# Three of four activation chunks transposed by DMA instead of by TensorE, in a fused spectral filter and GEGLU kernel

## The chip, the cores and the metric

The kernel runs on one core of one Trainium2 chip. The metric is the device time of one execution in microseconds (us); the median of three runs of the kernel before is 183.36 us (182.89 to 183.69). The core has five engines that each work through their own list of instructions in order and wait for each other through semaphores: TensorE (PE), ScalarE (ACT), VectorE (DVE), GpSimd (POOL) and SyncE (SP). SP only issues DMA transfers here; ACT issues a few as well.

## The reference, cut to what matters

```python
def _A_ref(x, w_r, w_i):                 # spectral filter
    X = jnp.fft.rfft2(x.astype(jnp.float32), axes=(-2, -1))
    X = X * (w_r + 1j * w_i)
    return jnp.fft.irfft2(X, s=(S, D), axes=(-2, -1)).astype(jnp.bfloat16)

def _B_ref(x, w_gate, w_up, w_down):     # GEGLU
    h = _gelu(jnp.einsum("bsd,df->bsf", x, w_gate)) * jnp.einsum("bsd,df->bsf", x, w_up)
    return jnp.einsum("bsf,fd->bsd", h, w_down)

xn = _layernorm(x, axis=-1)
return x + _A_ref(xn, A_w_r, A_w_i) + _B_ref(xn, B_w_gate, B_w_up, B_w_down)
```

S = 2048 rows, D = 512 columns, 1792 hidden columns; everything is stored as bfloat16.

## The kernel before, in words

The 2048 rows lie in 16 tiles j of 128 rows (one per partition) and 512 columns; four tiles make a chunk m (j = 4m to 4m+3). The layer norm of tile j (`ln_stats`, `ln_rstd`, `ln_apply`, line 425) leaves `xn[:, j, :]` in `bufA`. From there two branches start.

**GEGLU.** The matmuls need the rows on the free axis, so `transposes` (line 432) turns a chunk into `xnT`: for 4 tiles it is 16 TensorE transposes of 128x128 into PSUM (line 444), and then one copy by DVE (line 451) and one by ACT (line 453). `geglu_unit(b, fc)` (line 493) is 4 gate and 4 up matmuls (line 507), a gelu on ACT (line 519) and a product on DVE (line 527) for block b (one chunk of rows) and slice fc of the hidden columns. It waits for all the tiles of its chunk through `ev_xnT`. `down_unit` (line 541) multiplies a finished block by the down weights.

**Spectral branch.** POOL and DVE fold the columns (`half_fold`, `mirror_fold`) into `fold`, which lies in `bufB`. For each j, `unit_A` and `unit_d` do two small matrix products, ACT writes the result `T[:, j, :]` (line 611), which shares `bufA` with `xn`, and SP stores it to a scratch tensor in HBM (`stage_p`, line 613). When eight tiles are stored, `shuffle(q)` (line 616) reads them back in another order, in two transfers each. `unit_B`, `product` (with the two filters `wr_sb` and `wi_sb`), `unit_c`, a second scratch tensor and its read back (`back`), `unit_e` and `unit_fin` follow, and the last adds into `x_sb`.

**Order.** There is no planner: the program is one list written out by hand, and each engine takes its own instructions in the order of that list. `filler()` puts the next GEGLU or down unit between the spectral steps, so that TensorE has work all the time. Block 0 has its first six slices done ahead of the list of fillers. The three fillers ahead of the loop take slices 6 to 8 of block 0, those at j = 0 to 4 slices 9 to 13, and the filler at j = 5 is the first unit of block 1, `geglu_unit(1, 0)`, which is the first to need chunk 2 of the rows (j = 4 to 7). In words of the source, "chunk two" is m = 1, "chunk three" m = 2 and "chunk four" m = 3. The chunks two, three and four are transposed ahead of the loop, at j = 5 and at j = 9.

**The DMA list of SP.** All inputs come first (x, the weights w0 to w3, `small`, `fa`, the down weights `wd_sb` last). The ten transfers of the real filter (`load_filter("wr", ...)`, line 378) stand after the first store of `T` (at j = 1), those of the imaginary filter after the fifth (at j = 5). Of the ten, four bring 16 rows of 16 KB, four bring rows of 514 bytes in mirrored order, and two bring 16 rows of 514 bytes.

Of the kernel before, what the change touches and what calls it, by code (L numbers as in the profile page):

```python
# [7 lines left out]
ACT = mybir.ActivationFunctionType  # L8
# [9 lines left out]
P = 128  # L18
NJ = 16
# [13 lines left out]
def _build_constants():  # L33
# [20 lines left out]
    scale = 1.0 / (S * D)  # L54
    G = np.stack([2.0 * scale * q.T for q in quarters], axis=1)
    G[0, 0] *= 0.5
# [9 lines left out]
    for j in range(NJ):  # L66
# [3 lines left out]
        AM[:, j, 64] = alt  # L70
        EM[0:64, j, :] = 2.0 * np.cos(th.T)
        EM[64:128, j, :] = -2.0 * np.sin(th.T)
        EM[0, j, :] = 1.0
# [48 lines left out]
    for kind in range(2):  # L122
# [5 lines left out]
        for e2 in range(2):  # L128
            if kind == 1 and e2 == 0:
                wt = wi * np.conj(tw).T  # L130
                for base, z in ((0, wi), (2, wt)):
# [20 lines left out]
class _Sched:  # L152
# [14 lines left out]
    def total(self, stream):  # L167
        return (stream, self.stream_cnt[stream])
# [59 lines left out]
def bass_parallel_sum__spectral_gfnet__glu_gated_geglu__prompt_kernel(  # L228
# [19 lines left out]
    sch = _Sched()  # L248

    with ExitStack() as es:  # L250
# [5 lines left out]
        xnT = sb("xnT", [P, NDC, S])  # L256
# [5 lines left out]
        bufB = sb("bufB", [P, 4 * S])  # L262
        bufC = sb("bufC", [P, NG * (NK + 1)])
        tmp = sb("tmp", [P, 8 * NK])
        wr_sb = sb("wr_sb", [P, NG, NK])
        wi_sb = sb("wi_sb", [P, NG, NK])
# [16 lines left out]


        xn = bufA[:, :].rearrange("p (j c) -> p j c", j=NJ)
        T = xn
        ZT = bufA[:, :].rearrange("p (ci j q) -> p ci j q", ci=4, j=NJ)

        fold = bufB[:, :].rearrange("p (t s j d) -> p t s j d", t=2, s=2, j=NJ)
        V = bufB[:, :].rearrange("p (j c) -> p j c", j=NJ)  # L290

        half = bufC[:, 0:NJ * D].rearrange("p (m t j d) -> p m t j d", m=4, t=2, j=4)
# [26 lines left out]
        def sp_bank_bf(slot):  # L319
# [4 lines left out]
        ring_sp = _Ring((3, 4, 5, 6), bank_readers)  # L324
# [3 lines left out]
        ring_tr = _Ring((3, 4), bank_readers)  # L328

        streams = [("pe", 1), ("act", 1), ("dve", 1), ("pool", 1)]  # L330
        streams += [(n, 16) for n in ("x0", "x1", "x2", "x3", "xc1", "xc2", "xc3", "ident", "small", "fa", "eg", "wd", "wr", "wi",
                                      "w0", "w1", "w2", "w3", "dr0", "dr1", "perm1", "jx0", "jx1", "jx2", "jx3", "vd0_0", "vd0_1", "vd0_2", "vd1_0", "vd1_1", "vd1_2", "vd2_0", "vd2_1", "vd2_2", "vd3_0", "vd3_1", "vd3_2", "perm2", "out")]
        for name, inc in streams:
            sem = es.enter_context(nc.semaphore("sem_" + name))
            sch.add_stream(name, sem, inc)
        total = sch.total

        def load(stream, dst, src, eng="sp"):
            sch.op(eng, lambda e: e.dma_start(dst, src), stream=stream)  # L339
            return total(stream)  # L340
# [5 lines left out]
        spec = {}  # L346
# [29 lines left out]
        d2 = nc.dram_tensor("stage_g", [NG, P, NK], BF16).ap()  # L376

        def load_filter(name, dst, src):
            for ri in range(2):
                for e2 in range(2):  # L380
                    plus, minus = (slice(64 * ri + 2 * pm + e2, 64 * ri + 64, 4) for pm in range(2))
                    load(name, dst[plus, :, :], src.rearrange("(c h) k -> c h k", h=P)[:, 32 * e2:32 * e2 + 32, :])

                    g0 = 1 - e2
                    mirror = bass.AP(tensor=src.tensor, offset=src.offset + (P - 32 * e2 - g0) * NK,
                                     ap=[[P * NK, 16], [-NK, NG - g0], [1, NK]])
                    load(name, dst[minus, g0:NG, :], mirror)
                    if e2 == 0:
                        load(name, dst[minus, 0, :], src.rearrange("(c h) k -> c h k", h=P)[:, 64, :])
            spec[name] = [total(name)]  # L390

        def load_eg():
            sch.op("sp", lambda e: e.dma_start(eg[:], c_eg.ap()), deps=[spec["d_last"]], stream="eg")
            spec["eg"] = total("eg")


        ev_zero = sch.op("dve", lambda e: e.memset(hT[1][:, 0, 0:P], 0.0))
# [25 lines left out]
        ev_xn = {}  # L423
# [3 lines left out]
                                                             ALU.subtract, ALU.mult), deps=[ev_rstd[j], ev_ag[j]])  # L427

        ev_xnT = {}
        tr = {}  # L430

        def transposes(a, b, ring, per=2):

            n = (b - a) * P
            evs = []
            for h in range(NDC // per):
                slot, bdeps = ring.alloc(1)
                bank = sp_bank_bf(slot)[:, 0:per * n].rearrange("p (r s) -> p r s", r=per)

                def f_tr(e, h=h, bank=bank):  # L440
                    ins = None
                    for r in range(per):
                        for j in range(a, b):
                            ins = e.transpose(bank[:, r, (j - a) * P:(j - a + 1) * P],  # L444
                                              xn[:, j, (per * h + r) * P:(per * h + r + 1) * P], ident)
                    return ins

                ev_t = sch.op("pe", f_tr, deps=[ev_id] + [ev_xn[j] for j in range(a, b)] + bdeps)
                dst = xnT[:, per * h:per * h + per, a * P:b * P]
                if h % 2 == 0:  # L450
                    ev = sch.op("dve", lambda e, dst=dst, bank=bank: e.tensor_copy(dst, bank), deps=[ev_t])
                else:
                    ev = sch.op("act", lambda e, dst=dst, bank=bank: e.activation(dst, bank, ACT.Copy), deps=[ev_t])
                ring.add_reader(slot, ev)
                evs.append(ev)
            for j in range(a, b):
                ev_xnT[j] = evs
                tr[j] = ev_t

        ev_fold = {}  # L460

        ev_hf = {}

        def half_fold(m):

            rows = xn[:, 4 * m:4 * m + 4, :].rearrange("p j (h d) -> p h j d", h=2)
            deps = [ev_xn[j] for j in range(4 * m, 4 * m + 4)]
            ev_hf[m] = [sch.op("pool", lambda e, t=t, op=op: e.tensor_tensor(half[:, m, t, :, :], rows[:, 0, :, :], rows[:, 1, :, :], op), deps=deps)  # L468
                          for t, op in enumerate((ALU.add, ALU.subtract))]
# [99 lines left out]
        ev_T = {}  # L569
# [27 lines left out]
        def unit_d(j):  # L597
            slot, bdeps = ring_sp.alloc(1)

            def f_d(e):  # L600
                ins = None
                for r in range(4):
                    ins = e.matmul(sp_bank(slot)[:, AT[r] * P:(AT[r] + 1) * P], X1[j % NX1][:, r * P:(r + 1) * P], FD[:, r, :], start=True, stop=True)  # L603
                return ins

            ev_p = sch.op("pe", f_d, deps=[ev_X1[j], ev_fa] + bdeps)
            spec["d_last"] = ev_p
            X1_readers[j % NX1] = ev_p
            dst = T[:, j, :].rearrange("p (h m q) -> p q h m", h=2, q=2)
            src = sp_bank(slot).rearrange("p (h q m) -> p q h m", h=2, q=2)  # L610
            ev_T[j] = sch.op("act", lambda e: e.activation(dst, src, ACT.Copy), deps=[ev_p, tr[j]] + ev_hf[j // 4])  # L611
            ring_sp.add_reader(slot, ev_T[j])
            sch.op("sp", lambda e: e.dma_start(d1[j], T[:, j, :]), deps=[ev_T[j]], stream="dr%d" % (j // 8))
            spec["dr%d" % (j // 8)] = total("dr%d" % (j // 8))
# [86 lines left out]
        ev_ZT = {}  # L701
# [3 lines left out]
        def unit_e(j):  # L705
            slot, bdeps = ring_sp.alloc(1)

            def f_e(e):
                ins = None
                for ci in range(4):  # L710
                    ins = e.matmul(sp_bank(slot)[:, ci * P:(ci + 1) * P], V[:, j, V0[ci]:V0[ci] + HD - 1:2], EM[:, j, :], start=True, stop=True)  # L711
                return ins

            ev_p = sch.op("pe", f_e, deps=[spec["perm2"], spec["eg"]] + bdeps)
            src = sp_bank(slot).rearrange("p (ci q) -> p ci q", ci=4)
            ev_ZT[j] = sch.op("act", lambda e: e.activation(ZT[:, :, j, :], src, ACT.Copy), deps=[ev_p] + [spec["dr%d" % q] for q in range(2)])  # L716
            ring_sp.add_reader(slot, ev_ZT[j])

        ye_readers = [[], []]
# [88 lines left out]
        for j in range(4, 8):  # L808
            ln_apply(j)
        filler(2)  # L810
        transposes(4, 8, ring_tr)
        half_fold(1)

        beside = {
            0: ((ln_stats, 8), (ln_stats, 9)), 1: ((ln_stats, 10),), 2: ((ln_stats, 11), (mirror_fold, 1, 0)),
            3: ((ln_rstd, 8, 12), (mirror_fold, 1, 1)),
            4: tuple((ln_apply, i) for i in range(8, 12)) + ((half_fold, 2),),
            5: ((ln_stats, 12), (ln_stats, 13), (transposes, 8, 12, ring_sp)), 6: ((ln_stats, 14), (mirror_fold, 2, 0)),
            7: ((ln_stats, 15), (ln_rstd, 12, 16), (mirror_fold, 2, 1)),
            8: tuple((ln_apply, i) for i in range(12, 16)) + ((half_fold, 3),), 9: ((transposes, 12, 16, ring_sp),),  # L820
            10: ((mirror_fold, 3, 0), (mirror_fold, 3, 1), (clear_holes,), (shuffle, 0)),
        }
        for j in range(NJ):
            filler()
            unit_A(j)
            if j >= 1:
                unit_d(j - 1)
            if j == 1:
                load_filter("wr", wr_sb, A_w_r)
            if j == 5:  # L830
                load_filter("wi", wi_sb, A_w_i)
            for f, *args in beside.get(j, ()):
                f(*args)
        filler()
# [83 lines left out]
```

## Time and profile before

| | |
|---|---|
| median of 3 runs | 183.36 us |
| the profiled execution, its own time | 182.99 us |
| its span in the profile | 181.2 us |
| PE busy | 175.1 us of the span |
| DVE, ACT, POOL busy | 117.3, 88.5, 55.5 us |
| moved by DMA | 26.10 MB |
| granted TensorE clock | 1.00 |

The profile is of one execution on the chip; "span" is the time from its first to its last instruction, and the device time has 1.8 us around it. PE busy 97% of the span means that nearly everything else lies beside matmuls. "To landing" is the time from the issue of a transfer until its data has arrived.

### The profile page before, as it was taken

How to read it: one execution, taken by the hardware profiler on the slowest of the kernel's cores; microseconds unless marked ns; L12 is line 12 of the kernel's file. 1: busy time of each engine (PE TensorE's matmuls, PEld its weight loads, DVE VectorE, ACT ScalarE, POOL GpSimd, SP SyncE). 2: the span in 40 equal slices, each digit the busy share in tenths (PEclk: the TensorE clock that was granted, in tenths of full speed). 3: DMA queues.
4: the chain of work that ended last, by engine and by line, in shares of the span. 5: the costliest groups of instructions: out<-in, count | busy, mean ns of one | idle time of the engine just before them, and what ended most of it. 6: DMA issues, size and time to landing. Idle time of an engine off the chain costs nothing.

```text
span 181.2 us, 3176 instructions
## 1 busy us (share of the span) xinstructions
PE 175.1 (97%) x1148; PEld 99.8 (55%) x1168; DVE 117.3 (65%) x252; ACT 88.5 (49%) x161; POOL 55.5 (31%) x54
## 2 busy tenths in 40 slices
PE   7889999999999999999999999999999999999994
PEld 7778555565655554455455554444555555555453
DVE  3758958799675545538678585933266758886431
ACT  2744357777463542166576574523363636663000
POOL 0082290373630000000000000000049679997900
PEclk9999999999999999999999999999999999999999
DMA  5999970999999585723436858475001121110101
GB/s 153 354 364 374 371 250 30 187 195 195 208 205 201 156 257 157 220 58 98 112 87 131 204 113 215 103 168 116 5 0 58 37 75 36 58 60 5 58 29 58
DMA packets 32224, 26.10 MB, mean 144 GB/s; under 512 B 2256, under 2 KB 31440, under 8 KB 32080
## 3 DMA queue, kind: packets, MB, share of 16 engines
q1 hardware_dynamic: 28368, 23.90, 50.2%
q10 hardware_dynamic: 3840, 2.00, 5.3%
q8 instruction: 9, 0.15, 0.4%
q14 instruction: 7, 0.06, 0.1%
HBM read 17.48 MB, written 6.30 MB: 131 GB/s over the span
## 4 chain that ended last, share of the span: by engine, by line
PE 90%; DMA 4%; DVE 3%; SPq 1%; issue 1%
PE ps L507 50%; PE ps L555 27%; DMA wu_sb<-in_B_w_up_dram 4%; PE ps L577 2%; PE ps L732 2%; PE ps L711 2%; PE ps L603 2%; PE ps L649 2%; PE ps L680 2%; PE ps L444 2%; SPq L339 1%; DVE hT L527 1%; DVE tmp L666 1%; DVE tmp L668 0%; DVE JX L667 0%
## 5 line engine op out<-in xcount | busy, mean ns | idle before, releaser
L507 PE MATMUL ps<-xnT,wu_sb 128*128 128x512 bf16 (+1 forms) x246 | 58.3, 358 | 0.1
L507 PE MATMUL ps<-xnT,wg_sb 128*128 128x512 bf16 (+1 forms) x234 | 56.2, 357 | 1.3 <-DMA wu_sb<-in_B_w_up_dram 0.5
L527 DVE TENSOR_TENSOR hT<-ps,gg 128x512 bf16<-128x512 f32 (+1 forms) x62 | 39.5, 638 | 21.7 <-PE ps L507 20.5
L555 PE MATMUL ps<-wd_sb,hT 128*128 128x512 bf16 (+1 forms) x234 | 50.3, 366 | 0.2
L519 ACT ACTIVATE gg<-ps 128x512 bf16<-128x512 f32 (+1 forms) x62 | 34.4, 555 | 25.4 <-PE ps L507 24.3
L746 POOL TENSOR_TENSOR bufC<-bufC 128x256 bf16<-128x256 f32 x16 | 14.7, 917 | 85.5 <-DVE bufC L743 85.5
L507 PEld LDWEIGHTS ps<-xnT,wu_sb 128*128 128x128 bf16 x248 | 24.2, 98 | 24.2
L555 PEld LDWEIGHTS ps<-wd_sb,hT 128*128 128x128 bf16 x238 | 22.9, 98 | 22.6
L507 PEld LDWEIGHTS ps<-xnT,wg_sb 128*128 128x128 bf16 x248 | 22.9, 98 | 16.0 <-DMA wu_sb<-in_B_w_up_dram 0.7
L561 DVE TENSOR_TENSOR x_sb<-ps,x_sb 128x512 bf16<-128x512 f32 (+1 forms) x17 | 11.2, 660 | 28.7 <-PE ps L555 28.7
L750 POOL TENSOR_TENSOR x_sb<-x_sb,bufC 128x512 bf16<-128x512 bf16 x16 | 18.7, 1170 | 2.3
L468 POOL TENSOR_TENSOR bufC<-bufA 128x1024 bf16<-128x1024 bf16 x8 | 16.8, 2125 | 7.9 <-DVE bufA L426 7.9
L611 ACT ACTIVATE bufA<-ps 128x512 bf16<-128x512 f32 x16 | 11.9, 744 | 9.2 <-PE ps L603 9.2
L685 ACT ACTIVATE Vp<-ps 128x514 bf16<-128x514 f32 x16 | 9.6, 599 | 13.6 <-PE ps L680 13.6
L716 ACT ACTIVATE bufA<-ps 128x512 bf16<-128x512 f32 x16 | 9.4, 597 | 13.5 <-PE ps L711 13.5
L403 DVE BATCH_NORM_STATS2 st<-x_sb 128x6 f32<-128x512 bf16 x16 | 10.9, 678 | 2.2 <-DMA x_sb<-in_A_x_dram 2.2
L742 DVE TENSOR_TENSOR bufC<-bufC,ps 128x256 f32<-128x256 f32 x16 | 6.7, 421 | 5.3 <-ACT bufC L739 5.3
L654 ACT ACTIVATE Xc<-ps 128x514 bf16<-128x514 f32 x12 | 7.0, 595 | 4.0 <-PE ps L649 4.0
L418 POOL TENSOR_SCALAR rstd<-ag 128x4 f32<-128x4 f32 (+1 forms) x4 | 1.6, 402 | 20.2 <-DVE ag L404 20.2
L584 ACT ACTIVATE tmp<-ps 128x512 bf16<-128x512 f32 x9 | 5.4, 597 | 4.5 <-PE ps L577 4.5
L739 ACT ACTIVATE bufC<-ps 128x256 f32<-128x256 f32 x16 | 6.0, 378 | 2.6 <-PE ps L732 2.6
L746 DVE TENSOR_TENSOR bufC<-bufC 128x256 bf16<-128x256 f32 x16 | 6.8, 425 | 0.5
(46 smaller groups left out, 144.1 us busy)
## 6 DMA issues: line engine op xcount, KB each, us to landing
stage_g<-Vp SPq DMA_DIRECT2D x16, 128.5 KB, 2.8
stage_p<-bufA SPq DMA_DIRECT2D x16, 128.0 KB, 7.5
bufC<-stage_p SPq DMA_DIRECT2D x4, 512.0 KB, 5.1
out_dram<-x_sb SPq DMA_DIRECT2D x15, 128.0 KB, 1.7
wd_sb<-in_B_w_down_dram SPq DMA_DIRECT2D x1, 1792.0 KB, 14.0
wr_sb<-in_A_w_r_dram SPq DMA_DIRECT2D x6, 257.0 KB, 6.5
wi_sb<-in_A_w_i_dram SPq DMA_DIRECT2D x6, 257.0 KB, 11.0
JX<-Xc SPq DMA_DIRECT2D x24, 64.2 KB, 2.3
```

The lines of the kernel that those rows point to most:

```text
L403: ev = sch.op("dve", lambda e: e.bn_stats(st[:, j, :], x_sb[:, j, :]), deps=[ev_x[j]])
L468: ev_hf[m] = [sch.op("pool", lambda e, t=t, op=op: e.tensor_tensor(half[:, m, t, :, :], rows[:, 0, :, :], rows[:, 1, :, :], op), deps=deps ...
L507: ins = e.matmul(gu_bank(slot)[:, 0:w], wsb[:, dc, fc * P:(fc + 1) * P], xnT[:, dc, b * 512 + a:b * 512 + a + w], start=(dc == 0), stop=(d ...
L519: ev_gg = sch.op("act", lambda e: e.activation(gg, gu_bank(gslot)[:, 0:w], ACT.Gelu_apprx_tanh), deps=[ev_gm] + gg_readers[s2])
L527: ev_h = sch.op("dve", lambda e: e.tensor_tensor(hT[hb][:, fc, a:a + w], gu_bank(uslot)[:, 0:w], gg, ALU.mult), deps=[ev_um, ev_gg] + hdeps)
L555: ins = e.matmul(bank(slot)[:, 0:w], hT[hb][:, fc, jj * P:(jj + 1) * P], wd_sb[:, fc, cs], start=(fc == 0), stop=(fc == NFC - 1))
L561: ev_a = sch.op("dve", lambda e, slot=slot, cs=cs: e.tensor_tensor(x_sb[:, j, cs], bank(slot)[:, 0:w], x_sb[:, j, cs], ALU.add), deps=[ev_ ...
L611: ev_T[j] = sch.op("act", lambda e: e.activation(dst, src, ACT.Copy), deps=[ev_p, tr[j]] + ev_hf[j // 4])
L685: ev_v = sch.op("act", lambda e: e.activation(Vp[sv][:], sp_pair(slot), ACT.Copy), deps=[ev_p] + Vp_readers[sv])
L716: ev_ZT[j] = sch.op("act", lambda e: e.activation(ZT[:, :, j, :], src, ACT.Copy), deps=[ev_p] + [spec["dr%d" % q] for q in range(2)])
L746: y = [sch.op(("dve", "pool")[h], lambda e, h=h, op=op: e.tensor_tensor(rS[s2][:, h * HD:(h + 1) * HD], yeS[s2][:, 0, :], yeS[s2][:, 1, :] ...
L750: ev_o = sch.op("pool", lambda e: e.tensor_tensor(x_sb[:, j, :], x_sb[:, j, :], rS[s2], ALU.add), deps=[a, b, ev_xn[j]] + ev_acc.get(j, []))
```

## The change

The chunks two to four are no longer transposed by TensorE but by DMA transfers that SP issues, one for each tile of 128x512, from `xn` to `xnT`. The first four stand ahead of the loop, where the 16 TensorE transposes of chunk two stood. The others are spread over j = 5 to 10, so that all twelve are issued ahead of `shuffle(0)`. Chunk one stays on TensorE.

`T` moves from `bufA` to `bufB`, where each tile takes the place of the folded tile that `unit_A` has read, and the order of dimensions of `fold` changes to make the two match. With it the wait of the `T` write for the transposes and the folds goes away. The final `ZT`, still in `bufA`, waits for the transfers of the three chunks instead of for the stores.

The real filter is loaded directly behind the down weights, in place of after the first store of `T`; the imaginary filter's ten transfers follow the first four transposes, two at each j from 0 to 4.

```diff
-        fold = bufB[:, :].rearrange("p (t s j d) -> p t s j d", t=2, s=2, j=NJ)
+        fold = bufB[:, :].rearrange("p (j t s d) -> p t s j d", t=2, s=2, j=NJ)
+        T = bufB[:, :].rearrange("p (j c) -> p j c", j=NJ)
...
+        for _ in load_filter("wr", wr_sb, A_w_r):
+            pass
...
+        def transfers(a, b):
+
+            for j in range(a, b):
+                sch.op("sp", lambda e, j=j: e.dma_start(xnT[:, :, j * P:(j + 1) * P], xn[:, j, :], transpose=True),
+                       deps=[ev_xn[j]], stream="tr%d" % (a // 4))
+            for j in range(a, b):
+                ev_xnT[j] = [total("tr%d" % (a // 4))]
...
-            ev_T[j] = sch.op("act", lambda e: e.activation(dst, src, ACT.Copy), deps=[ev_p, tr[j]] + ev_hf[j // 4])
+            ev_T[j] = sch.op("act", lambda e: e.activation(dst, src, ACT.Copy), deps=[ev_p])
...
-            ev_ZT[j] = ...  deps=[ev_p] + [spec["dr%d" % q] for q in range(2)])
+            ev_ZT[j] = ...  deps=[ev_p] + [ev_xnT[i][0] for i in (7, 11, 15)])
...
-        transposes(4, 8, ring_tr)
+        transfers(4, 8)
         half_fold(1)
+        filter_i = load_filter("wi", wi_sb, A_w_i)
...
-            5: ((ln_stats, 12), (ln_stats, 13), (transposes, 8, 12, ring_sp)), 6: ((ln_stats, 14), (mirror_fold, 2, 0)),
-            7: ((ln_stats, 15), (ln_rstd, 12, 16), (mirror_fold, 2, 1)),
-            8: tuple((ln_apply, i) for i in range(12, 16)) + ((half_fold, 3),), 9: ((transposes, 12, 16, ring_sp),),
-            10: ((mirror_fold, 3, 0), (mirror_fold, 3, 1), (clear_holes,), (shuffle, 0)),
+            5: ((ln_stats, 12), (ln_stats, 13), (transfers, 8, 9)), 6: ((ln_stats, 14), (mirror_fold, 2, 0), (transfers, 9, 10)),
+            7: ((mirror_fold, 2, 1), (ln_stats, 15), (ln_rstd, 12, 16), (transfers, 10, 11)),
+            8: tuple((ln_apply, i) for i in range(12, 16)) + ((half_fold, 3), (transfers, 11, 12)),
+            9: ((transfers, 12, 14),), 10: ((transfers, 14, 16), (mirror_fold, 3, 0), (mirror_fold, 3, 1), (clear_holes,), (shuffle, 0)),
...
-            if j == 1:
-                load_filter("wr", wr_sb, A_w_r)
-            if j == 5:
-                load_filter("wi", wi_sb, A_w_i)
+            for _ in range(2):
+                next(filter_i, None)
```

`load_filter` becomes a generator that yields after each transfer. The list of SP in the changed kernel reads: inputs, down weights, ten transfers of the real filter, four transposing transfers, then the imaginary filter and the stores of `T` in turn, the remaining eight transposing transfers between the stores of j = 4 to 9, `shuffle(0)`, the last six stores, `shuffle(1)`.

More of the change, by code (lines that the diff above doesn't have):

```diff
@@ L285, in bass_parallel_sum__spectral_gfnet__glu_gated_geglu__prompt_kernel @@
         xn = bufA[:, :].rearrange("p (j c) -> p j c", j=NJ)
-        T = xn
         ZT = bufA[:, :].rearrange("p (ci j q) -> p ci j q", ci=4, j=NJ)
-        fold = bufB[:, :].rearrange("p (t s j d) -> p t s j d", t=2, s=2, j=NJ)
+        fold = bufB[:, :].rearrange("p (j t s d) -> p t s j d", t=2, s=2, j=NJ)
+        T = bufB[:, :].rearrange("p (j c) -> p j c", j=NJ)
         V = bufB[:, :].rearrange("p (j c) -> p j c", j=NJ)
@@ L331, in bass_parallel_sum__spectral_gfnet__glu_gated_geglu__prompt_kernel @@
         streams += [(n, 16) for n in ("x0", "x1", "x2", "x3", "xc1", "xc2", "xc3", "ident", "small", "fa", "eg", "wd", "wr", "wi",
-                                      "w0", "w1", "w2", "w3", "dr0", "dr1", "perm1", "jx0", "jx1", "jx2", "jx3", "vd0_0", "vd0_1", "vd0_2", "vd1_0", "vd1_1", "vd1_2", "vd2_0", "vd2_1", "vd2_2", "vd3_0", "vd3_1", "vd3_2", "perm2", "out")]
+                                      "w0", "w1", "w2", "w3", "dr0", "dr1", "perm1", "jx0", "jx1", "jx2", "jx3", "vd0_0", "vd0_1", "vd0_2", "vd1_0", "vd1_1", "vd1_2", "vd2_0", "vd2_1", "vd2_2", "vd3_0", "vd3_1", "vd3_2", "perm2", "tr1", "tr2", "tr3", "out")]
         for name, inc in streams:
@@ L382, in load_filter @@
                     load(name, dst[plus, :, :], src.rearrange("(c h) k -> c h k", h=P)[:, 32 * e2:32 * e2 + 32, :])
+                    yield
                     g0 = 1 - e2
@@ L387, in load_filter @@
                     load(name, dst[minus, g0:NG, :], mirror)
+                    spec[name] = [total(name)]
+                    yield
                     if e2 == 0:
                         load(name, dst[minus, 0, :], src.rearrange("(c h) k -> c h k", h=P)[:, 64, :])
-            spec[name] = [total(name)]
+                        yield
         def load_eg():
@@ L429, in bass_parallel_sum__spectral_gfnet__glu_gated_geglu__prompt_kernel @@
         ev_xnT = {}
-        tr = {}
         def transposes(a, b, ring, per=2):
@@ L457, in transposes @@
                 ev_xnT[j] = evs
-                tr[j] = ev_t
+        def transfers(a, b):
[4 more added lines that the diff above has]
+                ev_xnT[j] = [total("tr%d" % (a // 4))]
         ev_fold = {}
@@ L715, in unit_e @@
             src = sp_bank(slot).rearrange("p (ci q) -> p ci q", ci=4)
-            ev_ZT[j] = sch.op("act", lambda e: e.activation(ZT[:, :, j, :], src, ACT.Copy), deps=[ev_p] + [spec["dr%d" % q] for q in range(2)])
+            ev_ZT[j] = sch.op("act", lambda e: e.activation(ZT[:, :, j, :], src, ACT.Copy), deps=[ev_p] + [ev_xnT[i][0] for i in (7, 11, 15)])
             ring_sp.add_reader(slot, ev_ZT[j])
```

## The prediction

> **What bounds the kernel now.** I read the page's busy times first, then the chain that ended last, piece by piece in order of time.
>
> ```profile
> PE 175.1 (97%) x1148; PEld 99.8 (55%) x1168; DVE 117.3 (65%) x252; ACT 88.5 (49%) x161; POOL 55.5 (31%) x54
> ...
> PE 90%; DMA 4%; DVE 3%; SPq 1%; issue 1%
> ...
> 23.97 0.89 PE ps L444 x16
> ...
> 37.68 0.89 PE ps L444 x16
> ...
> 48.74 0.89 PE ps L444 x16
> ```
>
> TensorE is the bound, 97% of the span, and 90% of the last chain is its work. The three bottom lines (start, length) are the transposes of chunks two, three and four: they stand on the path themselves. Whatever leaves TensorE shortens the time, and whatever makes it wait lengthens it, for there is no slack behind it.
>
> Next is when the first unit of block 1 starts, which is the first reader of chunk two. The timeline of TensorE has the fillers of j = 0 to 4 up to 34.9 us, and then:
>
> ```profile
> 34.90 0.39 PE L577 MATMUL ps<-fa,bufB 128*128 128x128 bf16 x4
> 35.12 0.39 PE L603 MATMUL ps<-fa,tmp 128*128 128x128 bf16 x4
> 35.34 1.03 PE L507 MATMUL ps<-xnT,wg_sb 128*128 128x512 bf16 x4
> ```
>
> The last line is `geglu_unit(1, 0)`. Then the transfers: SP's issues by the timeline, the DMA share (second to last column) and rate in GB/s (last) by stretches, and times to landing.
>
> ```profile
> 13.84 0.44 SPq L339 DMA_DIRECT2D wd_sb<-in_B_w_down_dram  x1
> 30.06 0.32 SPq L613 DMA_DIRECT2D stage_p<-bufA  x1
> 30.42 6.45 SPq L339 DMA_DIRECT2D wr_sb<-in_A_w_r_dram  x10
> 36.91 2.17 SPq L613 DMA_DIRECT2D stage_p<-bufA  x4
> ...
> wd_sb<-in_B_w_down_dram SPq DMA_DIRECT2D x1, 1792.0 KB, 14.0
> ...
> 25.00:26.00 1.00, 1.00 (x7) 0.41 (x6) 0.30 (x1) 1.00 (x2) 1.00 (x2) 1.00 0.85 267
> 26.00:27.00 1.00, 0.95 (x8) 0.61 (x8) 0.37 (x1) 0.56 (x2) 1.00 (x1) 1.00 0.14 44
> ...
> 34.00:36.00 2.00, 2.00 (x17) 1.14 (x16) 1.11 (x3) 1.51 (x4) 0.04 (x1) 1.00 1.09 170
> ...
> wr_sb<-in_A_w_r_dram SPq DMA_DIRECT2D x1, 257.0 KB, 9.0
> stage_p<-bufA SPq DMA_DIRECT2D x1, 128.0 KB, 8.3
> ```
>
> The down weights land at 13.84 + 14.0 = 27.8 us, and the engines fall idle at about 26.1. The filter then moves at only 170 GB/s, though the share is 1.09 (packets in flight overlap, so it can pass 1): the engines are not short of work but slow at this work. The last two lines belong to the tenth filter transfer, issued at 36.3, and to the store issued next, at 36.91: they land at 45.3 and 45.2. A lone store of that size, the one of 30.06, lands in 1.7 us by its own window. So a transfer waits behind everything issued ahead of it on SP's queue.
>
> How long does a filter occupy the queue? The first transfer of `wr_sb` lands at 30.42 + 3.8 = 34.2, the tenth at 45.3, so nine take 11.1 us. By the windows around each issue the 16 KB-row kind follows its predecessor by about 1.0 us, the mirrored one by about 1.7, the 8 KB one by about 0.6. With 1.0 for the first, a filter costs 12.1 us of queue. The imaginary one confirms it, though it had stood in the queue for 8 us when its turn came: behind stores that end at 38.6 + 7.7 = 46.3, its last lands at 46.1 + 12.4 = 58.5, or 12.2 us.
>
> **The change, part by part.**
>
> *Transposes taken from TensorE.* 48 instructions in three pieces of 0.89 us, all on the path: 3 x 0.89 = -2.67 us. Three copies each of DVE (about 0.68) and ACT (1.02) go too; both engines are idle a third of the time or more and end no long wait of TensorE, so 0.
>
> *`T` to `bufB`, `fold` reordered.* The `T` copy (744 ns) keeps its shape; the eight `mirror_fold` (674 ns) write runs of 128 in place of 512. If that doubled them, 0.7 us each would still fit, since DVE waited 20.5 us in all for TensorE ahead of its products. 0. The waits that the `T` write loses had long ended.
>
> *Real filter moved up.* It fills the gap between 26.1 and 30.4 us. Its ten issues (about 0.6 us each) go out by 13.84 + 0.44 + 6.45 = 20.7 if the queue takes them, ahead of the readiness of chunk two: DVE writes tiles 4 to 7 from 21.54 to 22.9. But the transposes of chunk two are now behind the filter in the queue. The filter runs from 26.1 and its last transfer lands at 27.8 + 12.1 = 39.9 us. Before, TensorE had chunk two at 24.9 and read it from 35.34; with the first piece of 0.89 gone it wants it at 34.45. **The filter alone lands 5.45 us too late.**
>
> *The twelve transposing transfers.* The trace shows none. Each moves 128 KB within SBUF. The lower bound is a plain store of that size: the four of 36.91 land between 45.2 and 46.3, so 0.37 us each. The nearest small-piece row is the mirrored filter transfer: 16 x 31.5 rows of 514 bytes, 31.5 for each of 16 engines, in 1.7 us, or 54 ns a piece. A 128x512 tile in 128-column pieces is 512 pieces of 256 bytes, 32 an engine. At half a piece's time (by bytes) it is 0.87 us, at a whole one 1.73. I take the middle, 1.3 us. Above these, the 8 KB transfer holds the queue 0.6 us with a single piece per engine; if each of the four 128-column groups paid that, it is 2.4 us. Moving single elements at 54 ns would be 65,536 / 16 x 54 ns = 221 us each; I think that excluded for a transfer that is told to transpose, and give it 1 in 100.
>
> At 1.3 us the fourth lands at 39.9 + 5.2 = 45.1, and TensorE waits 45.1 - 34.45 = **+10.65 us**. With 0.37 it is 6.9, with 2.4 it is 15.05. SP's own issue of a transpose is also unknown, but the first four have 15 us (22.9 to 38) of cover while the filter drains.
>
> Two rules of the Trainium skill disagree here, and no run so far shows the operation. "VectorE: DVE Perf Modes", The three transpose paths, gives 1309 ns for one 128x128 by DMA against 390 ns on TensorE (here 55.6 ns in a stream); four blocks in a row would be an estimated 5.2 us a transfer and a time near 212 us. "Advanced Engine Details and Errata", X-Bar Transpose (TRN2), says that such transfers are as fast as regular ones, which is the 0.37 us row and 189.6 us.
>
> *A cold restart.* At the start, after idleness, the 50 warm-up matmuls of 128x128 took 4.81 us, while 16 transposes of that size take 0.89, 55.6 ns each. So 4.81 - 2.78 = 2.0 us went to a slow start, though the granted clock reads 1.00. Whether a wait of 10 us in the middle brings it back the trace doesn't show: bounds 0 and 2.0. I take **+2.0**, the only row of a start after idleness.
>
> The skill's "TensorE: Matmul & The Clock Gate", Why this matters for your kernels, warns of gaps over about 3 us, after which the clock is halved again. It would make the full 2.0 of this wait, and nothing of a wait under 3.
>
> *What is late next.* Behind the waiting unit on TensorE stand `unit_A(5)` and `unit_d(4)`, hence the store of tile 4 on SP, and with it the transfers of chunks three and four. Chunk three is read at block 2's start, some 18 fillers later (about 79 us before), chunk four at block 3's: covered by over 15 us. The tighter one is `shuffle(1)`: issued at 68.43, its second half landed at 75.5, and `unit_B` began at 76.98: 1.5 us of slack. At 1.3 us a transfer the queue holds chunk two to 43.4, the imaginary filter and four stores to 57.1, eight transposes and six stores (10.4 + 2.2) to 69.7, `shuffle(0)` (5.1 - 1.7 = 3.4) to 73.1. The last `T` is then written at 66.7 - 2.67 + 10.65 + 2.0 = 76.7, so its store finds the queue free. +0.
>
> **Sum.** 182.99 - 2.67 + 10.65 + 2.0 = 192.97 us for the profiled execution; its time lies 0.37 under the median, so 193.3 us.
>
> **Rivals.**
>
> *Slow transposes, a second wait.* At 2.4 us each the first wait is 15.05 us, and the queue is behind: chunk two to 47.8, filter and stores to 61.4, eight transposes and six stores to 82.8, `shuffle(0)` to 86.2, six stores land at 90.1, `shuffle(1)` 7.1 us later at 97.2. `unit_B` would be due at 76.98 - 2.67 + 15.05 + 2.0 = 91.4: 5.8 us more. 183.36 - 2.67 + 15.05 + 2.0 + 5.8 = 203.5. It begins near 2 us a transfer. For it: nothing measured; against it: the mirrored row. 0.20.
>
> *Faster.* The filter follows the weights at their rate (350 GB/s between 22 and 25 us): 2.05 MB in 5.9 us, landed at 33.7, transposes of 0.37 us at 35.2, a wait of 0.7: 183.36 - 2.67 + 0.7 = 181.4. It decides from chunk two landing before 34.45 + 2.67 = 37.1. Against it: both filters took 12 us with nothing else to slow them. It could also come about if transposes overtake in the queue; the store behind the filter did not. 0.07.
>
> *No change.* Chunk two at about 37.1 us; it needs half of each of these errors. 0.03.
>
> **How the numbers follow.** The forecast has 0.70, with its own range from 187.6 (0.37 us, no cold start) to 197. The range goes from 186.5, a filter that takes 11 us as well, to 205, to take in most of the slow rival. Less than 0.5% either way can't be told from no change. Faster 0.07, same 0.03, slower 0.90.
>
> **What would show it.** Right: a wait of some 7 to 12 us on TensorE at about 34.5 us, ended by the transfers into `xnT`; real filter landing near 40; every later stage shifted by the net amount, with matmuls after the wait at twice their time for 2 to 4 us. Wrong: chunk two landed by 37 us; transposes far from 1.3 us apart; or a second wait at the first `unit_B`.

## The result, and the profile after

The changed kernel takes 190.16 us (median of 4 runs, 189.64 to 190.69) against 183.36 us for the kernel before (median of 3 runs; a fourth took 312.61 us): a ratio of 1.0374 with a 95% interval of 1.032 to 1.0428. Here and below, medians and ranges are over all runs of a kernel but for that one, while ratios leave out runs over 1.5% above the kernel's fastest. The prediction was 193.3 us, slower.

The page of the changed kernel first, with the lines that answer to those shown of before.

```profile
span 187.9 us, 3106 instructions
...
PE 175.6 (93%) x1120; PEld 98.0 (52%) x1120; DVE 115.5 (61%) x249; ACT 85.9 (46%) x158; POOL 55.1 (29%) x54
...
PE 88%; DVE 5%; DMA 3%; SPq 2%; issue 1%; ACT 0%
```

48 transposes are gone (1168 weight loads before, 1120 now), and TensorE's share fell from 97% to 93%. The two busy times, 175.1 and 175.6 us, can't be compared: the page of before shows only 1148 matmuls beside its 1168 weight loads, so about 20 records are missing there. The timeline of TensorE shows where (start, length, instructions, and in brackets the idle time ahead with what ended it).

```profile
34.33 0.39 PE L616 MATMUL ps<-fa,tmp 128*128 128x128 bf16 x4
42.09 1.89 PE L520 MATMUL ps<-xnT,wg_sb 128*128 128x512 bf16 x4 [7.37 <-DMA xnT<-bufA]
43.77 1.91 PE L520 MATMUL ps<-xnT,wu_sb 128*128 128x512 bf16 x4
45.48 0.63 PE L590 MATMUL ps<-fa,bufB 128*128 128x128 bf16 x4
45.91 0.43 PE L616 MATMUL ps<-fa,tmp 128*128 128x128 bf16 x4
46.18 1.03 PE L520 MATMUL ps<-xnT,wg_sb 128*128 128x512 bf16 x4
47.04 1.03 PE L520 MATMUL ps<-xnT,wu_sb 128*128 128x512 bf16 x4
47.90 0.39 PE L590 MATMUL ps<-fa,bufB 128*128 128x128 bf16 x4
48.13 0.39 PE L616 MATMUL ps<-fa,tmp 128*128 128x128 bf16 x4
48.35 1.03 PE L520 MATMUL ps<-xnT,wg_sb 128*128 128x512 bf16 x4
```

The first unit of block 1 waits 7.37 us for chunk two. From its start to the start of the next unit it is 46.18 - 42.09 = 4.09 us; the one behind that takes 48.35 - 46.18 = 2.17. So 1.92 us more go to slow matmuls. The windows show why (the number after the engines' is the granted clock, then DMA share and GB/s).

```profile
36.00:38.00 2.00, 0.00 (x0) 0.00 (x0) 0.29 (x1) 0.00 (x0) 1.63 (x1) 1.00 1.30 151
38.00:40.00 2.00, 0.00 (x0) 0.00 (x0) 0.00 (x0) 0.00 (x0) 2.00 (x2) 0.79 1.56 74
...
42.00:44.00 2.00, 1.91 (x5) 0.74 (x6) 0.00 (x0) 0.00 (x0) 0.00 (x0) 0.50 0.96 200
44.00:46.00 2.00, 2.00 (x9) 0.97 (x8) 0.28 (x1) 0.60 (x1) 0.00 (x0) 0.50 1.25 246
46.00:48.00 2.00, 2.00 (x16) 1.06 (x14) 1.93 (x5) 1.69 (x3) 0.00 (x0) 1.00 1.04 230
```

The clock falls to half after about 4.4 us of waiting and comes back about 4 us after work resumes. Together: 7.37 + 1.92 - 2.67 = 6.62 us; the span grew by 187.9 - 181.2 = 6.7. Only 0.1 us is left over. SP's issues in the timeline, the time to landing of the last filter transfer, and the chain of waits over the end of the wait:

```profile
14.20 14.61 SPq L339 DMA_DIRECT2D wr_sb<-in_A_w_r_dram  x10
28.85 11.69 SPq L468 DMA_TRANSPOSE xnT<-bufA  x4
40.59 1.23 SPq L339 DMA_DIRECT2D wi_sb<-in_A_w_i_dram  x2
...
wr_sb<-in_A_w_r_dram SPq DMA_DIRECT2D x1, 257.0 KB, 11.9
```

```profile
36.30 0.79 SPq L468
37.09 0.04 issue
37.14 2.10 SPq L468
39.23 0.04 issue
39.28 2.77 DMA xnT<-bufA
42.05 0.05 issue
42.09 1.03 PE ps L520 x2
```

The ten filter transfers keep SP until 28.8 us, not 20.7, and the four transposes until 40.5: SP is held up. It doesn't wait for data, since DVE had written chunk two by 23.0 us. That it waits until the queue has room is the likely reading, but the trace doesn't name what it waits for. The last filter transfer, issued at 28.2, lands 11.9 us later, at 40.1; the last transpose lands at 42.05.

### The profile page after: what moved, and what is told of

It reads as the page before. It is cut to its first block, busy times and chain, and to the rows that moved or that the text cites. A ratio compares the mean times of both kernels' runs of the same rounds, so it can differ in the third digit from the quotient of the medians.

```text
span 187.9 us, 3106 instructions
## 1 busy us (share of the span) xinstructions
PE 175.6 (93%) x1120; PEld 98.0 (52%) x1120; DVE 115.5 (61%) x249; ACT 85.9 (46%) x158; POOL 55.1 (29%) x54
## 2 busy tenths in 40 slices
DMA packets 38752, 27.67 MB, mean 147 GB/s; under 512 B 8784, under 2 KB 37968, under 8 KB 38608
## 4 chain that ended last, share of the span: by engine, by line
PE 88%; DVE 5%; DMA 3%; SPq 2%; issue 1%; ACT 0%
PE ps L520 51%; PE ps L568 26%; PE ps L745 2%; PE ps L724 2%; PE ps L590 2%; PE ps L662 2%; PE ps L616 2%; PE ps L693 2%; DMA x_sb<-in_A_x_dram 2%; SPq L468 2%; DMA xnT<-bufA 1%; DVE hT L540 1%; DVE bufA L433 1%; DVE st L410 1%; DVE tmp L679 1%
## 5 line engine op out<-in xcount | busy, mean ns | idle before, releaser
L520 PE MATMUL ps<-xnT,wg_sb 128*128 128x512 bf16 (+1 forms) x248 | 59.4, 362 | 7.5 <-DMA xnT<-bufA 7.4
L520 PE MATMUL ps<-xnT,wu_sb 128*128 128x512 bf16 (+1 forms) x248 | 59.4, 362 | 0.0
L540 DVE TENSOR_TENSOR hT<-ps,gg 128x512 bf16<-128x512 f32 (+1 forms) x62 | 39.4, 637 | 29.5 <-PE ps L520 28.1
L624 ACT ACTIVATE bufB<-ps 128x512 bf16<-128x512 f32 x16 | 11.9, 743 | 9.2 <-PE ps L616 9.2
L729 ACT ACTIVATE bufA<-ps 128x512 bf16<-128x512 f32 x16 | 9.4, 597 | 13.4 <-PE ps L724 13.4
L590 PEld LDWEIGHTS ps<-fa,bufB 128*128 128x128 bf16 x64 | 5.1, 101 | 4.1 <-issue 0.6
```

What stands on the lines that cost most here:

```text
L520: ins = e.matmul(gu_bank(slot)[:, 0:w], wsb[:, dc, fc * P:(fc + 1) * P], xnT[:, dc, b * 512 + a:b * 512 + a + w], start=(dc == 0), stop=(d ...
L540: ev_h = sch.op("dve", lambda e: e.tensor_tensor(hT[hb][:, fc, a:a + w], gu_bank(uslot)[:, 0:w], gg, ALU.mult), deps=[ev_um, ev_gg] + hdeps)
```

## The experiments

The theory after the result: chunk two waits because the filter's 2.05 MB stand ahead of it on SP's queue. Four kernels were made to test it, all run on one chip beside the kernel before (183.06 us).

**Filters back where they were, transposes by DMA.**

```diff
-        for _ in load_filter("wr", wr_sb, A_w_r):
-            pass
...
-            for _ in range(2):
-                next(filter_i, None)
+            for at, name, dst, src in ((1, "wr", wr_sb, A_w_r), (5, "wi", wi_sb, A_w_i)):
+                if j == at:
+                    for _ in load_filter(name, dst, src):
+                        pass
```

> Queue theory (chunk two waits because the real filter's 2.05 MB stand ahead of it on SP's queue): with both filters loaded where they were before the change, the four transposing transfers run directly behind the down weights, at about 0.5 us each, and land by 30 us; TensorE wants them at 34.7, so the wait of 7.4 us and the slow matmuls after it (1.9 us) are gone and the three pieces of 0.89 us stay saved: 183.4 - 2.7 = 180.7 us. Rival (transposing transfers are slow in themselves, some 3 us each as the 11.7 us of SP's issue suggests): chunk two lands at 37 to 39, a wait of 2 to 4 us stays, 183 to 185 us.

Measured: 191.22 us, ratio 1.0442 (1.0406 to 1.0479). The wait for chunk two is gone, as expected (it landed at 32.05 us, not by 30, and was wanted at 34.7), but the gain didn't come. TensorE's waits in this kernel:

```profile
PE ps L658 <- DMA bufC<-stage_p: 7.7, 1, 7.7
```

Line 658 is `unit_B`: it now waits 7.7 us for `shuffle(1)`, and the clock reads 0.50 after that too. There is a second wait that the first had hidden.

**The real filter's move alone**, on the kernel before.

```diff
-            if j == 1:
-                load_filter("wr", wr_sb, A_w_r)
...
+        load_filter("wr", wr_sb, A_w_r)
+
         def load_eg():
```

> The kernel before with nothing changed but the real filter loaded behind the down weights (all transposes on TensorE). Queue theory: no reader on the path waits for anything behind the filter, so 183.4 us within 0.5%, with the filter landing near 40 us. Rival (the filter's loads themselves disturb the stream of weights, which land at 29.6 in place of 27.8): above 185 us.

Measured: 183.12 us, ratio 1.0005 (0.9995 to 1.0015). The move costs nothing by itself; it needs a reader behind it.

**Chunk two alone back on TensorE.**

```diff
-        transfers(4, 8)
+        transposes(4, 8, ring_tr)
```

> The changed kernel with chunk two alone back on TensorE; chunks three and four stay with the transfers, the real filter stays behind the down weights. Queue theory: no wait at 34.7 us, two pieces of 0.89 us saved: 183.4 - 1.8 = 181.6 us. Rival (the eight later transfers also cost, through SP's queue and the shuffle): 183 us or more, with a wait at the first unit_B.

Measured: 182.74 us, ratio 0.9985 (0.9969 to 1.0001): between the two expectations. There is no wait at 34.7 us, but 1.2 us at the first `unit_B`. The rival was right that the eight later transfers cost something.

**Chunk two's transposes and the real filter swapped on SP's list**, nothing else.

```diff
         transfers(4, 8)
+        for _ in load_filter("wr", wr_sb, A_w_r):
+            pass
         half_fold(1)
```

> The changed kernel with the four transposing transfers of chunk two and the ten transfers of the real filter swapped on SP's list, nothing else. Queue theory: as with the filters put back, 180.7 us, with the real filter landing near 42 us and nobody waiting for it. Rival (slow transposes): 183 to 185 us. Rival (early filter harms by itself): above the time with the filters put back by 1 us or more.

Measured: 190.29 us (187.94 to 191.19), ratio 1.0315 (1.026 to 1.037). Of the waits, the one for chunk two is gone, and one of 5.0 us stands at `unit_B`. That settles the first wait: order on the queue alone makes or removes it. The profile is of the shortest of the four runs, so in the others the second wait may have been longer. The second is seen in SP's list, here the kernel before and then the swapped one (the two halves of `shuffle(0)`, the last six stores of `T`, `shuffle(1)`):

```profile
59.42 1.30 SPq L622 DMA_DIRECT2D bufC<-stage_p  x2
60.77 6.28 SPq L613 DMA_DIRECT2D stage_p<-bufA  x6
68.43 1.24 SPq L622 DMA_DIRECT2D bufC<-stage_p  x2
```

```profile
49.05 2.98 SPq L464 DMA_TRANSPOSE xnT<-bufA  x1
...
61.95 2.50 SPq L464 DMA_TRANSPOSE xnT<-bufA  x2
64.58 2.12 SPq L631 DMA_DIRECT2D bufC<-stage_p  x2
66.74 5.11 SPq L622 DMA_DIRECT2D stage_p<-bufB  x6
73.97 1.23 SPq L631 DMA_DIRECT2D bufC<-stage_p  x2
```

`shuffle(0)` goes out 5.2 us later, and `shuffle(1)`, which needs the last stores, 5.5 us later. The last `T` was written at 64.7 us, but its store left SP only at 71.42 (in the kernel before 66.69 and 66.72), so the delay stands on SP's list. TensorE wanted the data at 75.2 and could start at 80.1. A transposing transfer takes SP 1.2 us where a store takes about 0.6. Two explanations: SP's own time (theory S), or the load on the queue and the DMA engines (theory D). Four more kernels, beside 183.3 us of the kernel before:

**Chunk four's transfers behind `shuffle(1)`**, chunk two ahead of the filter.

```diff
-            9: ((transfers, 12, 14),), 10: ((transfers, 14, 16), (mirror_fold, 3, 0), ...
+            10: ((mirror_fold, 3, 0), ...
...
         shuffle(1)
+        transfers(12, 16)
         load_eg()
```

> The kernel with chunk two's transfers ahead of the real filter, and chunk four's four transfers moved behind shuffle(1), where SP is free and 30 us remain until they are read. Theory S (the second wait, 5.0 us at the first unit_B, comes from SP's own time: 1.25 us to issue a transposing transfer, twelve of them ahead of the last store of T and of shuffle(1)): four fewer ahead take 5 us off SP, shuffle(1) goes out near 69 us and the wait falls to 0 to 1 us: 180.7 to 181.7 us. Rival D (the DMA engines are behind with the bytes, the filters above all): the eight transposes moved 1 MB only, the wait stays at 4 us or more, 186 us.

Measured: 184.6 us with a wide spread (182.55 to 187.07), ratio 1.0052 (1.002 to 1.0083). In the profiled execution (183.03 us) `shuffle(0)` goes out at 59.60 us and the wait at `unit_B` is gone. But the four transposes hold SP for 7.14 us from 69.81, the transfers into `JX` behind them go out late, and `unit_c` waits 1.74 us. The wait at `unit_B` went as theory S expected and not as rival D did, and the time fits neither. It doesn't decide between the two, since four transfers fewer are also 0.5 MB less on the queue. The other runs took 1.6 us more in the median, which this profile doesn't explain.

**Plain copies in place of the eight later transposes** (the transposition of chunks three and four is left out).

```diff
-                sch.op("sp", ... e.dma_start(xnT[:, :, j * P:(j + 1) * P], xn[:, j, :], transpose=True),
+                src = xn[:, j, :] if j < 8 else xn[:, j, :].rearrange("p (r s) -> p r s", r=NDC)
+                sch.op("sp", ... e.dma_start(..., src, transpose=True) if j < 8 else e.dma_start(..., src),
```

> The kernel with chunk two's transfers ahead of the real filter, but the eight transfers of chunks three and four are plain copies of the same 128x512 elements in the same 256-byte pieces to the same place: the transposition of 1024 rows is left out. Theory S: a plain issue takes SP about 0.58 us in place of 1.25, 8 x 0.67 = 5.4 us less ahead of shuffle(1), and the wait at the first unit_B is gone: 180.7 us. Rival D (bytes and pieces on the DMA engines): the same load, so the wait stays at 4 us or more and the time at 186 us or above.

Measured: 186.59 us, ratio 1.0178 (1.012 to 1.0237). The wait stays:

```profile
PE ps L659 <- DMA bufC<-stage_p: 4.8, 1, 4.8
...
62.35 1.32 SPq L632 DMA_DIRECT2D bufC<-stage_p  x2
63.71 5.87 SPq L623 DMA_DIRECT2D stage_p<-bufB  x6
72.89 1.23 SPq L632 DMA_DIRECT2D bufC<-stage_p  x2
```

SP reaches `shuffle(0)` only 2.2 us earlier than with transposes, though eight issues at half the time should have saved about 5, and `shuffle(1)` 1.1 us earlier. Theory S, as the whole cause, falls: the same bytes in the same pieces, not transposed, make nearly the same wait.

**Idle matmuls during the wait**, on the changed kernel: 125 of 128x128, whose result nobody uses.

```diff
+            if j == 5:
+                keep_warm(125)
             filler()
```

> The changed kernel with 125 idle matmuls of 128x128 (7 us at 55.6 ns, their result is not used) put on TensorE just ahead of the unit that waits for chunk two. Theory (the clock falls to half after the wait of 7.4 us, which costs 1.9 us): the granted clock stays at 1.00, the eight matmuls of the unit take 1.73 us in place of 3.4, and the time falls by 1.9 us to about 188.3 us. Rival (the matmuls are slow because of the transfers into the same memory, not because of the idle time): no gain, 190.2 us or above.

Measured: 191.5 us, ratio 1.0443 (1.0385 to 1.0501): no gain, so the expectation failed. The timeline says why:

```profile
34.73 7.14 PE L843 MATMUL ps<-hT 128*128 128x128 bf16 x125
44.26 1.04 PE L520 MATMUL ps<-xnT,wg_sb 128*128 128x512 bf16 x4 [2.38 <-DMA xnT<-bufA]
45.13 1.59 PE L520 MATMUL ps<-xnT,wu_sb 128*128 128x512 bf16 x4
...
47.36 1.77 PE L520 MATMUL ps<-xnT,wg_sb 128*128 128x512 bf16 x4
48.97 1.03 PE L520 MATMUL ps<-xnT,wu_sb 128*128 128x512 bf16 x4
```

Chunk two landed 2.2 us later in this execution, and 2.38 us of idleness were left. Of the 2.2 us, 0.7 are the filter's (landed at 40.82) and 1.5 the third transpose's, which came 2.0 us behind the second (on this see the last section). The unit starts at full speed, and the clock falls to 0.50 a microsecond into it, for about 3.5 us. The slow phase came all the same, only later: this unit and the next take 6.02 us, to 50.28, in place of 4.34, so 1.7 us are lost. The rival (transfers slow the matmuls) isn't supported: the first four ran at full speed, and in the kernel with the filters put back the clock reads 0.50 after a wait with no transposing transfer near it. What the warm clock is worth was not isolated; the 1.92 us are read from the trace.

**Chunks two and four by DMA, chunk three on TensorE**, filters as before the change.

```diff
-            5: (..., (transfers, 8, 9)), 6: (..., (transfers, 9, 10)), 7: (..., (transfers, 10, 11)),
+            5: (..., (transposes, 8, 12, ring_sp)), 6: (...), 7: (...),
...
         shuffle(1)
+        transfers(12, 16)
```

> Filters where they were before the change, chunk two by transfers directly behind the down weights, chunk four by transfers behind shuffle(1), chunk three on TensorE. No transfer stands between the stores of T. Theory S: no wait at either place, two pieces of 0.89 us saved, 183.1 - 1.8 = 181.3 us. Rival D: the backlog of the filters is as in the kernel before, so the same 181.3 us; what would tell against both is a wait at the first unit_B of over 1 us.

Measured: 183.79 us, ratio 1.0042 (1.0022 to 1.0063). The wait at `unit_B` is 0.3 us, as expected, but the four transfers behind `shuffle(1)` again make `JX` late and `unit_c` waits 2.16 us, which takes the 1.8 us back.

A last group, beside 183.1 us of the kernel before.

**Chunk four from ACT's queue**, one transfer behind each of four GEGLU units, chunk two ahead of the filter.

```diff
             negate(i)
+            sch.op("act", lambda e, j=j4: e.dma_start(xnT[...], xn[:, j, :], transpose=True),
+                   deps=[ev_xn[j4], ev_xnT[11][0]], stream="tr3")
```

> As with chunk two's transfers ahead of the real filter, but chunk four's four transfers are issued by ACT, one behind each of the four GEGLU units after the last store of T, where ACT idles 1 to 3 us a unit, so that SP's list holds only eight transposes and nothing between shuffle(1) and the JX transfers. Theory D (SP's one queue is late: what stands ahead of shuffle(0) and of JX, bytes and issue time together, sets the second wait): no wait of over 1 us at the first unit_B nor at the first unit_c, 180.6 to 181.6 us. Rival (the transposes on the DMA engines beside the shuffle are what makes it late, whoever issues them): a wait of 1.5 us or more stays, 182.5 us or above.

Measured: 185.75 us, ratio 1.0102 (1.0071 to 1.0132). In the profiled execution (187.07 us) SP is free of the four, and yet `unit_B` waits 3.4 us: the last store lands 3.38 us after its issue in place of 1.7, beside the transposes of ACT. The profiled run was among the longer of six (184.29 to 187.64), so these sizes stand for that run, but none of the six came near the expected 180.6 to 181.6 us. The rival's bounds held: issuing from ACT didn't take the wait away.

**The same, but chunk two on TensorE** and the filter behind the down weights.

> Chunk two on TensorE, the real filter behind the down weights, chunk three by SP in the loop, chunk four by ACT as above. Theory D: four fewer transposes ahead of shuffle(0) than with chunk two alone on TensorE, so its wait of 1.2 us goes and two pieces of 0.89 us stay saved: 183.3 - 1.8 = 181.5 us, 0.5 to 1 us above the kernel with all three by transfers if that one has no wait. Rival as above: 182.5 us or more.

Measured: 182.07 us, ratio 0.9934 (0.9921 to 0.9947): the one version that is clear of noise faster than the kernel before, if only by 0.7%. The chain ahead of `unit_B`, in a profiled run of 183.11 us, the longest of six (the others took 181.61 to 182.11):

```profile
64.59 0.75 ACT bufB L624
65.34 0.02 issue
65.36 1.99 DMA stage_p<-bufB
67.35 0.02 issue
67.36 0.53 SPq L635
67.89 0.04 issue
67.93 9.07 DMA bufC<-stage_p
```

Now the last `T` is stored and shuffled as soon as it is there, but the shuffle lands 9.07 us after issue beside the transposes of ACT, where it took 6.5 before the change. `unit_B` waits 1.28 us in this run; what the five others, 1 us or more shorter, waited, no profile shows.

**All filter rows read whole** (the mirrored reading is left out, as many bytes), otherwise as the swapped kernel.

```diff
-                    load(name, dst[minus, g0:NG, :], mirror)
+                    load(name, dst[minus, :, :], src.rearrange("(c h) k -> c h k", h=P)[:, 32 * e2:32 * e2 + 32, :])
```

> The kernel with chunk two's transfers ahead of the real filter and all twelve ahead of shuffle(0), but every filter transfer brings whole rows of 16 KB: the mirrored reading of half of the filter rows is left out, as many bytes are loaded. A filter then takes about 8 x 1.0 = 8 us of the queue in place of 12.1. Theory D (the second wait of 5.0 us comes from the backlog on SP's queue, to which the filters' mirrored rows add some 8 us): the wait at the first unit_B falls by 3 us or more, 182 to 184 us. Theory S (it is the time SP needs to issue twelve transposes): the wait stays at about 5 us, 187 us or above.

Measured: 185.69 us, ratio 1.0143 (1.0123 to 1.0163). The wait falls from 5.0 to 2.9 us: towards theory D, but by less than the 3 us expected. A transfer of whole rows took about 1.3 us and not 1.0, so a filter took 10.3 us (32.32 to 42.61) and not 8. The filters' backlog is a part of the second wait, not all of it.

**Chunk four between the last six stores**, from SP, with chunk two on TensorE.

```diff
+            11: ((transfers, 12, 13),), 12: ((transfers, 13, 14),), 13: ((transfers, 14, 15),), 14: ((transfers, 15, 16),),
```

> Chunk two on TensorE, the real filter behind the down weights, chunk three's four transfers in the loop as changed, and chunk four's four issued by SP behind shuffle(0), one between each two of the last six stores of T, where SP waits for ACT some 4 us in all. Theory D: shuffle(0) goes out as early as with chunk four on ACT (near 56 us), the last store of T is at most 1 us later than its data, and nothing stands beside shuffle(1), which lands in 6 us in place of 9.1: no wait of over 0.5 us at the first unit_B, 183.1 - 1.8 = 181.3 us or 0.5 to 1 us less than with ACT. Rival (four transposes anywhere between 56 us and the landing of shuffle(1) cost 1 us or more): 182 us or above.

Measured: 182.98 us, ratio 0.9987 (0.9966 to 1.0007). `shuffle(0)` goes out at 55.47 us, and the shuffle lands in 6.3 us, but the last store goes out at 68.0, 2.7 us later than with chunk four on ACT (65.36), and `unit_B` waits 0.95 us. The rival's bound held.

## Why the prediction was right

The main step, that chunk two would stand behind the filter and TensorE would wait for it, was right, and the swap shows that order on the queue is the cause. By its terms:

- *Taken from TensorE, -2.67 us.* Right: with it the sum above closes to 0.1 us.
- *Filter landing at 39.9 us.* Measured 40.1. Its premise that SP would issue everything by 20.7 us was wrong (it was held until 28.8), which changed nothing, since order on the queue is what counts.
- *Transposing transfers, 1.3 us each.* **This is the mis-sized term.** From the filter's landing to the fourth transfer's it is 42.05 - 40.1 = 1.95 us, about 0.5 each, near the lower bound of 0.37 and not at the small-piece row of 0.87 to 1.73. It made the forecast wait 10.65 us in place of 7.37, which is all of the 3.1 us by which the forecast was too high. By the prediction's own list, transposes far from 1.3 us apart were a sign of being wrong. The 0.5 us isn't a fixed price: with the same four ahead of the filter, in the swapped kernel, they took 4.5 us from the weights' landing, 1.1 each (last section). Of the two pages weighed, the measurement sides with "Advanced Engine Details and Errata", X-Bar Transpose (TRN2); the figure of "VectorE: DVE Perf Modes" for one block would have given ten times the occupancy seen here.
- *Cold restart, +2.0 us.* Measured 1.92, with a granted clock of 0.50 that was not in the trace of before. Choosing 2.0 from bounds of 0 and 2.0 was in part luck, as the prediction had one row to go by, from the start of the program. The clock of 1.00 that it read there rests on no record: the trace's first entry for the clock is at 4.68 us.
- *What is late next, +0.* True for this kernel and for a weaker reason than given. `shuffle(1)` was issued at 75.13 us and its second half landed near 81.7, ahead of `unit_B` at 83.67. But it was on time only because TensorE itself came 6.7 us later. The prediction counted the eight other transposes in the queue but not the time that SP takes over them, and with it the late stores; with the first wait removed a second of 5.0 to 7.7 us stands at `unit_B`.

So the rival "slow transposes, a second wait" had the right place for the wrong reason: the transposes are fast in the queue, and the second wait exists, hidden behind the first. For the rival "faster", chunk two landing in time is not enough by itself: the swapped kernel, where it did, still takes 190.29 us (its other condition, a filter at the weights' rate, no run met). The first wait is shown. Of the second it is shown that it needs neither the transposition as such nor the early filter, and that from 5.0 us it shrinks with four transfers fewer ahead of `shuffle(0)` (to 0 with chunk four's later, to 1.2 with chunk two's on TensorE) and with faster filters (to 2.9 us), each read in one profiled run; how it divides between SP's held-up queue and the busy DMA engines stays open.

## What to carry to other kernels

Work moved from the bounding engine to DMA takes its place in a queue: before crediting the saving, list what stands ahead of it on that queue and when that drains, and then what stands behind it. Removing the wait that a trace shows can uncover one of the same size behind it, so a fix is judged by its own trace and not by the length of the wait removed. Of twelve transposing transfers only the eight latest-needed paid here, with the last four off SP's list: 0.7%, where their two pieces of 0.89 us promise 1.0% and all three 1.5%.

## What the runs showed of the hardware

A transposing transfer of 128x512 within SBUF lands 2.4 us after issue when alone, against 1.7 for a plain store of that size, and takes SP about 1.2 us to issue. Twelve of them add 38,752 - 32,224 = 6,528 packets, 544 each: 512 of 256 bytes and 32 of 4 bytes.

Transposing transfers were also late, by 0.7 to 1.7 us, where the program's code was being loaded. In the swapped kernel chunk two's four landed at 28.18, 29.54, 30.01 and 32.21 us. Here is the rate in GB/s in the last of these gaps, from 29.5 to 30.9 us in 40 slices, with one of the queues that were at work in it:

```profile
GB/s 307 278 300 285 300 285 278 1635 507 963 4700 0 0 0 0 0 0 0 0 0 0 0 0 0 0 0 0 0 0 0 0 0 0 0 0 0 0 45 162 647
...
q8 instruction: 1, 0.02, 5.0%
```

The second line is a load of 16 KB of instructions at 29.76 us; from 29.9 us on nothing else starts for 0.9 us. Counted from 0.5 us behind the predecessor or 2.45 us after the issue, whichever is later, 19 transposing transfers of SP in all the traces landed over 0.5 us late, and each had such a load, of 8 or 16 KB, in the 3.2 us ahead. That is a coincidence in time; no run tested the cause.

The clock of TensorE fell to half after waits of 7.71, 7.37, 4.96, 4.78, 3.38 and 2.93 us, and after 2.38 us behind 7 us of small matmuls on zeros; after waits of 1.74 and 2.16 us it stayed at 1.00. The warning about gaps of over 3 us in "TensorE: Matmul & The Clock Gate", Why this matters for your kernels, is thus about right here, with the cases of 2.93 and 2.38 us below it. In these traces a stretch between two changes of the clock lasts a whole multiple of 3.41 us (34.13 and 6.83 us in the changed kernel, 71.68 and 10.24 with the filters put back, 40.96 and 3.41 with the idle matmuls). So it also counts where a wait falls: the clock fell at the end of steps of 3.41 us in which TensorE had idled for 2.2 us or more (2.21 of the 2.38 us), and stayed where it was 1.74 or less (the 2.16 us lay half in one step, half in the next). This was read from the traces and not tested.

Kernels with transposing transfers beside stores vary more from run to run (182.55 to 187.07 us for one of them) than the kernel before (182.92 to 183.98 on the same chip). Why isn't known.
